# The first unit's loads and roots in whole pieces, the last store on GpSimd's queue, and a longer list of rank shifts

## The chip, the cores and the metric

The kernel runs on one core of a Trainium2 chip. TensorE (PE) multiplies matrices, VectorE (DVE) and ScalarE (ACT) work elementwise, GpSimd (POOL) and SyncE (SP) mostly issue DMAs; ACT can issue DMAs too. The metric is device time in microseconds; the kernel before took 703.22 us (median of 3 runs, 700.52 to 704.69).

## The reference, cut to what matters

Two blocks run one after the other. The first is a gated linear recurrence over 4 batches x 8 heads x 768 steps x 48 channels with a complex decay `a`, whose magnitude is limited first; the second is a dense block with a squared ReLU on the 3072 x 384 result.

```python
mag = np.sqrt(a_re * a_re + a_im * a_im)
scale = np.minimum(mag, 0.999) / (mag + 1e-06)
a_re_n, a_im_n = a_re * scale, a_im * scale
for t in range(S):                       # complex state S_re, S_im per head, 48 x 48
    new_re = ar * S_re - ai * S_im
    new_im = ar * S_im + ai * S_re
    S_re, S_im = new_re + k_t v_t^T, new_im
    y[:, :, t] = q_t @ S_re
x = y as (3072, 384)
out = max(x @ w_in, 0) ** 2 @ w_out      # w_in 384 x 2048, w_out 2048 x 384
```

## The kernel before, in words

The 3072 rows are cut into six units of 512 rows. A unit `n` has these stages. `load(n)` (line 880) brings `a`, `q`, `k` into the tiles `aq` and `v` into `v`; the eight heads lie in two halves `z` of four heads each. `chain(n)` (line 921) limits the magnitude of `a` (`roots`, `normalise`), multiplies the decays up over four neighbouring steps (`inner`, the DVE lines 1011 to 1019), scans them over the whole sequence by a turn on PE (`totals`), DVE products (`scan`) and a turn back (`back`, copied out by ACT at line 1246), and multiplies `q` and `k` by the result (`rest`, with `inverse`, `factors`, `twist`, `squares` and `apply`). `pairs(n)` (line 1356) turns the products on PE, forms scores (line 1419), masks them on DVE (line 1422) and mixes them into the columns `xT`. `dense(n, grp)` (line 1503) multiplies `xT` by `w1` (line 1511), squares the ReLU on ACT (lines 1542, 1543) and multiplies by `w2` (line 1557 in unit 0, line 1619 later, where sums of `w2` in the tile `T` save one product in eight).

The weights are first fetched whole and converted in pieces of 768 columns: an ACT pass (line 830, for the later pieces a second one at line 834) and two or three DVE passes (lines 836, 840, 843). Unit 0 shares DVE and ACT with this conversion. The fetches wait for a small copy (`gate`, line 908) that waits for unit 0's `a`.

No engine's order is written by hand. `step(engine, duration, reads, writes, function, rank)` and `dma(...)` only list the steps; `Plan.order` (line 531) then walks through planned time and, on each engine, starts among the steps that are ready the one with the smallest rank, and among equals the one listed first. A rank is a pair such as `(CHAIN, n)`, made into a number by 100 times the first plus the second: pairs of unit n have about 100 + n, the chain 200 + n, dense and the fetches 300 + n. Where the planner sees PE without work it adds multiplications of the identity (line 735) to keep it busy. `plan.shift` (line 1759) adds numbers to single ranks: `single` by the step's number in the list, `groups` by the number of the group of steps with one engine, one source line and one rank. The instructions of an engine run in the order that comes out.

In unit 0, and for `z = 0` alone, `load` cuts the four heads into two halves `u` of two heads, so that `a_re` (on SP's queue) and `a_im` (on ACT's) come in two DMAs each, and `roots` (line 938) does its eight steps twice on 384 columns, once for each half. The loads of `q` and `k` of unit 0 are listed as reading `("a", 1)`.

The last rows of the output are stored in halves of 192 columns (`rows`, line 1566): three of the four on SP's queue, the very last one, `(i, half) == (1, 0)`, on ACT's.

Of the kernel before, what the change touches and what calls it, by code (L numbers as in the profile page):

```python
# [621 lines left out]
def fast_path(ctx, tc, q, k, v, a_re, a_im, moe_w_in, moe_w_out, out, flag):  # L622
# [7 lines left out]
    W = 4  # L630
# [117 lines left out]
    def ac(n):  # L748
        return n / 1200.0 + 0.18
# [120 lines left out]
    def parts(n):  # L870

        t, got = n * L, []
        while t < (n + 1) * L:
            b, s = divmod(t, S)
            m = min(S - s, (n + 1) * L - t)
            got.append(((t - n * L) // W, m // W, b, s))
            t += m
        return got

    def load(n):  # L880
        rank = (CHAIN, n)
        for half, name, pair in ((0, "a", (a_re, a_im)), (1, "qk", (q, k))):
            for z in range(2):
                t = aq[z][:, half * Z:(half + 1) * Z].rearrange(
                    "p (r h x) -> p r h x", r=2, h=HH)
                late = []
                if half and (n == 1 or n > 2):
                    late = [("xT", (n - 1) % 2, NM - 1)]
                if half and n == 0:
                    late = [("a", 1)]  # L890

                cut = 2 if n == 0 and half == 0 and z == 0 else 1
                for u in range(cut):
                    for j, ap in enumerate(pair):
                        for p0, m, b, s in parts(n):
                            hs = slice(u * HH // cut, (u + 1) * HH // cut)
                            src = ap[b, z * HH + hs.start:z * HH + hs.stop, s:s + m * W, :]
                            src = src.rearrange("h (p c) d -> p h (c d)", c=W)
                            queue = act if n == 0 and half == 0 and j else sp
                            dma(queue, late,  # L900
                                [(name, z)] + ([(name, z, "r", j, u)] if n == 0 else []),
                                lambda t=t, p0=p0, m=m, j=j, src=src, queue=queue, hs=hs:
                                queue.dma_start(out=t[p0:p0 + m, j, hs], in_=src),
                                rank, m * 3072 // cut, 4.0 if n else 3.0, group=n)
            if n == 0 and half == 0:
                for z in range(2):
                    step("POOL", 0.2, [("a", z)], [("gate",)],
                         lambda z=z: pool.tensor_copy(out=gate[:, z:z + 1],
                                                      in_=aq[z][:, Z - 1:Z]), rank)
        t = vv[vs(n)].rearrange("p (i h d) -> p i h d", i=W, h=H)  # L910
        for i in range(W):
            b, s = divmod(n * L + i * C, S)
            src = v[b, :, s:s + C, :].rearrange("h (t c) d -> c t h d", c=W)
            for c in range(W):
                vrank = (CHAIN, 1) if n == 1 else (DENSE, 6 + n)
                dma(pool, [("xT", (n - (vs(n) == vs(n - 1))) % 2, NM - 1)] if n else [("gate",)], [("v", vs(n))],
                    lambda i=i, c=c, src=src: pool.dma_start(  # L917
                        out=t[32 * c:32 * c + 32, i], in_=src[c]), vrank, 32 * 1536, 4.0,
                    group=n)

    def chain(n):
# [15 lines left out]

        def roots(z):
            f0, f1, m2, t = col[z]
            if n:  # L940
                check("ACT", ac(Z), [("a", z)], key(z, 0, 1), lambda: act.activation(
                    out=ff[z][:, 0:Z], in_=A[z], func=AF.Square,
                    accum_out=sums[:, n, z:z + 1]), first)
            cut = 2 if n == 0 and z == 0 else 1
            size = Y // cut
            for u in range(cut):
                def k(*js, u=u):
                    return key(z, *js) if n else [("f", z, j, u) for j in js]

                def part(x, u=u):  # L950
                    return x[:, ts(u, size)]
                if n == 0:

                    if z == 0:
                        step("ACT", ac(size), [("a", z, "r", 0, u)], k(0),
                             lambda u=u: act.activation(
                                 out=part(f0, u), in_=A[z][:, ts(u, size)], func=AF.Square), first)
                    for r in range(z == 0, 2):
                        def square(r=r, u=u):
                            x = A[z][:, r * Y + u * size:r * Y + (u + 1) * size]  # L960
                            dve.tensor_tensor(out=part(col[z][r], u), in0=x, in1=x, op=ALU.mult)
                        step("DVE", tt(size), [("a", z, "r", r, u)], k(r), square, first)
                step("DVE", tt(size), k(0, 1), k(2) + key(z, 2),
                     lambda u=u: dve.tensor_tensor(
                         out=part(m2, u), in0=part(f0, u), in1=part(f1, u), op=ALU.add), first)
                step("ACT", ac(size), k(2), k(0), lambda u=u: act.activation(
                    out=part(f0, u), in_=part(m2, u), func=AF.Ln), first)
                step("ACT", ac(size), k(0), k(1), lambda u=u: act.activation(
                    out=part(f1, u), in_=part(f0, u), func=AF.Exp, scale=-0.5), first)
                step("ACT", ac(size), k(1), k(3), lambda u=u: act.activation(  # L970
                    out=part(t, u), in_=part(f1, u), func=AF.Square), first)
                step("DVE", tt(size), k(2, 3), k(3), lambda u=u: dve.scalar_tensor_tensor(
                    out=part(t, u), in0=part(m2, u), scalar=-0.5, in1=part(t, u),
                    op0=ALU.mult, op1=ALU.mult), first)
                step("DVE", tt(size), k(1, 3), k(3) + key(z, 3),
                     lambda u=u: dve.scalar_tensor_tensor(
                         out=part(t, u), in0=part(t, u), scalar=1.5, in1=part(f1, u),
                         op0=ALU.add, op1=ALU.mult), first)

        def normalise(z):  # L980
            f0, f1, f2, t = col[z]
# [584 lines left out]
    def rows(n, grp, i, o, half=None):  # L1566
# [2 lines left out]
        final = n == NU - 1 and grp == 1  # L1569
        if final and half is None:  # L1570
            return
        queue = (act if (i, half) == (1, 0) else sp) if final else pool
        if final:
            sl = ts(half, DH)
            dma(queue, [("ot", o, half)], [], lambda: queue.dma_start(
# [179 lines left out]
    for i in range(2 * NPIECE):  # L1755
# [1 line left out]
    verdict()  # L1757

    plan.shift(
        groups={77: 100.01, 80: 2.93, 100: -0.9, 159: -2.64, 161: 0.18, 232: 0.28, 234: 103.28,  # L1760
            258: 1.25, 297: 0.64, 352: 0.34, 354: 0.6, 372: 0.17, 394: -2.31},
        single={368: 0.46, 613: -197.29, 866: 8.98, 921: 0.46, 1273: -97.94, 1425: -0.29,
            1687: -97.83, 1759: 1.33, 1763: 98.01})
    with tc.manual_schedule():
        bad = plan.emit(flag[0:1, 0:1])
    return bad
# [53 lines left out]
```

## Time and profile before

| what | value |
|---|---|
| median of 3 runs | 703.22 us (700.52, 703.22, 704.69) |
| the profiled execution's own time | 704.69 us |
| its span in the profile | 702.97 us; 1.72 us lie around it |
| PE busy | 686.7 us (98%), of which 62.5 us identity (line 735) |
| DVE / ACT / POOL busy | 572.7 / 350.4 / 174.7 us |
| granted PE clock | 1.00 in nearly all 20 us windows, 0.83 from 80 to 100 us |

All times are microseconds from the span's start. A line of a group names line of the kernel, engine, operation, output<-input tiles, number of columns and count. The chain of waits goes back from the last instruction, at each step to what released it. In a table by windows the columns are the stretch, its length, the busy time of PE, PE's weight loads (PEld), DVE, ACT and POOL with the instructions in parentheses, the granted PE clock, the DMA engines' busy share, and GB/s.

### The profile page before, as it was taken

How to read it: one execution, taken by the hardware profiler on the slowest of the kernel's cores; microseconds unless marked ns; L12 is line 12 of the kernel's file. 1: busy time of each engine (PE TensorE's matmuls, PEld its weight loads, DVE VectorE, ACT ScalarE, POOL GpSimd, SP SyncE). 2: the span in 40 equal slices, each digit the busy share in tenths (PEclk: the TensorE clock that was granted, in tenths of full speed). 3: DMA queues.
4: the chain of work that ended last, by engine and by line, in shares of the span. 5: the costliest groups of instructions: out<-in, count | busy, mean ns of one | idle time of the engine just before them, and what ended most of it. 6: DMA issues, size and time to landing. Idle time of an engine off the chain costs nothing.

```text
span 703.0 us, 12562 instructions
## 1 busy us (share of the span) xinstructions
PE 686.7 (98%) x4572; PEld 623.3 (89%) x4572; DVE 572.7 (81%) x1177; ACT 350.4 (50%) x582; POOL 174.7 (25%) x334
## 2 busy tenths in 40 slices
PE   9998999999999999999999999999999999999996
PEld 9998888667778999998998898999989989989995
DVE  6989989999889689997898598998689998337721
ACT  7575379955575534376424557333657242132230
POOL 6502543052300003205044050033230033032100
PEclk9999989999999999999999999999999999999998
DMA  9740459130530004735037570037550035288600
GB/s 283 216 176 19 116 133 310 56 68 23 158 114 23 1 19 122 190 91 145 6 97 194 124 154 12 1 95 184 136 150 1 24 90 139 59 289 279 202 7 22
DMA packets 56679, 79.58 MB, mean 113 GB/s; under 512 B 11008, under 2 KB 38784, under 8 KB 56608
## 3 DMA queue, kind: packets, MB, share of 16 engines
q0 software_dynamic: 15232, 40.72, 19.2%
q1 hardware_dynamic: 37088, 32.89, 18.2%
q10 hardware_dynamic: 4288, 5.08, 2.7%
q8 instruction: 38, 0.62, 0.4%
q14 instruction: 33, 0.27, 0.1%
HBM read 48.76 MB, written 4.72 MB: 76 GB/s over the span
## 4 chain that ended last, share of the span: by engine, by line
PE 67%; DVE 20%; ACT 3%; issue 3%; DMA 3%; POOL 2%; SPq 1%; DVEq 0%; ACTq 0%; POOLq 0%
PE d L1511 26%; PE d L1619 22%; PE sc L1419 5%; PE tr L1447 3%; PE yp L1471 3%; PE d L1557 2%; DVE f L1299 2%; DVE f L1285 2%; PE yp L1475 2%; DVE f L1011 2%; PE tr L1511 2%; POOL T L917 1%; PE sc L1511 1%; DVE aq L1289 1%; DVE w L840 1%
## 5 line engine op out<-in xcount | busy, mean ns | idle before, releaser
L1511 PE MATMUL d<-xT,w 128*128 128x256 f32 x1056 | 235.5, 380 | 0.7 <-DVE ot L1643 0.7
L1511 PEld LDWEIGHTS d<-xT,w 128*128 128x128 f32 x1056 | 198.8, 190 | 28.7 <-DVE ot L1643 1.5
L1619 PE MATMUL d<-w,g 128*128 128x192 f32 x768 | 132.8, 327 | 0.0
L1619 PEld LDWEIGHTS d<-w,g 128*128 128x128 f32 x768 | 124.9, 190 | 1.6 <-issue 0.9
L1542 ACT ACTIVATE g<-d 128x512 f32<-128x512 f32 x88 | 52.3, 594 | 127.9 <-PE d L1511 94.3
L1340 POOL DMA_DIRECT2D KC<-f x160 | 78.5, 498 | 110.9 <-issue 47.4
L1580 POOL DMA_DIRECT2D out_dram<-ot x22 | 12.6, 572 | 241.8 <-DVE ot L1643 146.4
L1619 PE MATMUL d<-T,g 128*128 128x192 f32 x384 | 66.5, 327 | 0.3 <-DVE g L1634 0.3
L735 PE MATMUL d<-ident 128*128 128x128 f32 x530 | 62.5, 282 | 1.5 <-POOL ident masks.py:199 1.5
L1619 PEld LDWEIGHTS d<-T,g 128*128 128x128 f32 x384 | 62.8, 190 | 0.8 <-DVE g L1634 0.6
L735 PEld LDWEIGHTS d<-ident 128*128 128x128 f32 x530 | 61.9, 198 | 1.5 <-POOL ident masks.py:199 1.5
L917 POOL DMA_DIRECT2D v<-in_v_dram x80 | 46.4, 587 | 65.5 <-PE yp L1471 30.5
L1543 ACT ACTIVATE g<-g 128x512 f32<-128x512 f32 x96 | 60.6, 631 | 3.1
L1634 DVE TENSOR_TENSOR g<-g 128x512 f32<-128x512 f32 x64 | 43.0, 683 | 22.2 <-ACT g L1543 15.7
L1419 PE MATMUL sc<-QT 96*128 96x128 f32 x368 | 48.0, 285 | 0.8 <-ACT QT L1405 0.8
L1481 ACT COPY yt<-yp 112x512 f32<-112x512 f32 x24 | 26.2, 1091 | 44.5 <-PE yp L1475 44.5
L1419 PEld LDWEIGHTS sc<-QT 96*128 96x128 f32 x368 | 45.0, 198 | 2.7 <-issue 1.3
L1285 DVE TENSOR_TENSOR f<-aq,xn 128x384 f32<-128x384 f32 (+1 forms) x64 | 45.1, 748 | 2.3 <-ACT xn L1246 2.3
L1299 DVE TENSOR_TENSOR f<-aq 128x384 f32<-128x384 f32 (+1 forms) x64 | 45.0, 751 | 0.6
L1557 PE MATMUL d<-w,g 128*128 128x384 f32 x128 | 44.2, 488 | 0.2 <-DVE w L843 0.2
L1422 DVE TENSOR_TENSOR A<-sc,mask 128x512 f32<-128x512 f32 x45 | 29.9, 681 | 14.6 <-PE sc L1419 14.6
L1011 DVE TENSOR_TENSOR f<-aq 128x384 f32<-128x384 f32 x72 | 36.8, 552 | 0.8
(195 smaller groups left out, 989.5 us busy)
## 6 DMA issues: line engine op xcount, KB each, us to landing
QT<-aq SPq DMA_DIRECT2D x128, 64.0 KB, 2.2
f<-in_moe_w_in_dram POOLq DMA_DIRECT2D x8, 768.0 KB, 7.2
f<-in_moe_w_out_dram POOLq DMA_DIRECT2D x8, 768.0 KB, 6.3
KC<-f POOLq DMA_DIRECT2D x104, 48.0 KB, 2.4
out_dram<-ot POOLq DMA_DIRECT2D x22, 192.0 KB, 2.3
QT<-aq ACTq DMA_DIRECT2D x64, 64.0 KB, 2.4
v<-in_v_dram POOLq DMA_DIRECT2D x80, 48.0 KB, 3.3
xT<-yt SPq DMA_DIRECT2D x36, 96.0 KB, 2.5
```

The source lines that it names most:

```text
L735: plan = Plan(lambda b: pe.matmul(bank[b][:, 0:C], lhsT=ident, rhs=ident, start=True, stop=True), ["d2", "d1", "d0"], lambda ap: tc.nc.val ...
L917: lambda i=i, c=c, src=src: pool.dma_start(out=t[32 * c:32 * c + 32, i], in_=src[c]), vrank, 32 * 1536, 4.0,
L1011: dve.tensor_tensor(out=f, in0=a[:, :, :, c - 1], in1=a[:, j, :, c].unsqueeze(1).to_broadcast([C, 2, HH, D]), op=ALU.mult)
L1285: lambda j=j, r=r: dve.tensor_tensor(out=f4[:, j, r], in0=a[:, r], in1=over(j), op=ALU.mult), late[z])
L1299: lambda j=j, r=r, o=o: dve.tensor_tensor(out=o[:, :, :, r * D:(r + 1) * D], in0=qk[:, j], in1=a[:, r], op=ALU.mult), late[z])
L1340: lambda i=i, c=c, queue=queue: queue.dma_start(out=kc[32 * c:32 * c + 32, i], in_=nat[32 * i:32 * i + 32, c]),
L1419: pe.matmul(sa[:, j], lhsT=T[:, j, 1, h], rhs=T[:, j, 0, h], start=True, stop=True)
L1511: pe.matmul(ps, lhsT=w1[:, f // FP, m, ts(f % FP, C)], rhs=xT[:, n % 2, m, ts(grp, G)], start=(m == 0), stop=(m == NM - 1))
L1542: act.activation(out=o, in_=ps, func=AF.Relu)
L1543: act.activation(out=o, in_=o, func=AF.Square)
L1557: pe.matmul(ps, lhsT=gt[:, f % 2, ts(i, C)], rhs=w2[:, f], start=(f == 0), stop=(f == NF - 1))
L1619: pe.matmul(bank[b][:, 0:DH], lhsT=g4[:, r, j], rhs=w(j), start=first and j == 0, stop=last and j == NT - 1)
```

## The change

It does four things.

1. `load`: unit 0's `a` for `z = 0` comes in one DMA for `a_re` and one for `a_im`, not two each; unit 0's `q` and `k` are no longer listed as reading `("a", 1)`; the planner's latency for these loads is 1.8 in place of 3.0.
2. `roots`: unit 0's `z = 0` is done in whole steps of 768 columns, like `z = 1`.
3. `rows`: the very last store is issued by POOL in place of ACT.
4. `plan.shift`: all 22 old entries stay, renumbered where ten steps fewer stand ahead of them, and 15 are added. By numbering the steps of the kernel before, the new ones touch: `groups` 51 (the two ACT copies of unit 0's `back`, rank 199.99 to 301.96), 183, 190, 192, 217 (unit 2: the first closing DVE step of `roots`, line 972; ACT's check at line 999, to the front; `joined` after line 1011, by +0.69; `twist`, line 1045, to the back), 396 and 411 (unit 5: `joined` and the first step of `inverse`, line 1033, to the front); `single` 48 (one DVE pass of the conversion, line 840), 244 (a turn of unit 0's second pair, line 1401), 425 and 481 (two PE steps of unit 0's dense, lines 1511 and 1557), 584 (a small DVE step of unit 1's `scan`), 731 (the DVE mask of unit 1's first pair, second head, line 1422, rank 101 to 204.3), 809 (the last of the sums of `w2`, rank 101.5 to 301.97), 2212 (an ACT check of unit 5, line 1258).

```diff
@@ load
-                if half and n == 0:
-                    late = [("a", 1)]
-
-                cut = 2 if n == 0 and half == 0 and z == 0 else 1
-                for u in range(cut):
-                    for j, ap in enumerate(pair):
-                        for p0, m, b, s in parts(n):
-                            hs = slice(u * HH // cut, (u + 1) * HH // cut)
-                            src = ap[b, z * HH + hs.start:z * HH + hs.stop, s:s + m * W, :]
-                            src = src.rearrange("h (p c) d -> p h (c d)", c=W)
-                            queue = act if n == 0 and half == 0 and j else sp
-                            dma(queue, late,
-                                [(name, z)] + ([(name, z, "r", j, u)] if n == 0 else []),
...
-                                rank, m * 3072 // cut, 4.0 if n else 3.0, group=n)
+                for j, ap in enumerate(pair):
+                    for p0, m, b, s in parts(n):
+                        src = ap[b, ts(z, HH), s:s + m * W, :].rearrange(
+                            "h (p c) d -> p h (c d)", c=W)
+                        queue = act if n == 0 and half == 0 and j else sp
+                        dma(queue, late, [(name, z)] + ([(name, z, "r", j)] if n == 0 else []),
+                            lambda t=t, p0=p0, m=m, j=j, src=src, queue=queue:
+                            queue.dma_start(out=t[p0:p0 + m, j], in_=src),
+                            rank, m * 3072, 4.0 if n else 1.8, group=n)
@@ roots
-            cut = 2 if n == 0 and z == 0 else 1
-            size = Y // cut
-            for u in range(cut):
...
-                step("DVE", tt(size), k(0, 1), k(2) + key(z, 2),
-                     lambda u=u: dve.tensor_tensor(
-                         out=part(m2, u), in0=part(f0, u), in1=part(f1, u), op=ALU.add), first)
...
+            step("DVE", tt(Y), key(z, 0, 1), key(z, 2), lambda: dve.tensor_tensor(
+                out=m2, in0=f0, in1=f1, op=ALU.add), first)
+            step("ACT", ac(Y), key(z, 2), key(z, 0), lambda: act.activation(
+                out=f0, in_=m2, func=AF.Ln), first)
+            step("ACT", ac(Y), key(z, 0), key(z, 1), lambda: act.activation(
+                out=f1, in_=f0, func=AF.Exp, scale=-0.5), first)
+            step("ACT", ac(Y), key(z, 1), key(z, 3), lambda: act.activation(
+                out=t, in_=f1, func=AF.Square), first)
+            step("DVE", tt(Y), key(z, 2, 3), key(z, 3), lambda: dve.scalar_tensor_tensor(
+                out=t, in0=m2, scalar=-0.5, in1=t, op0=ALU.mult, op1=ALU.mult), first)
+            step("DVE", tt(Y), key(z, 1, 3), key(z, 3), lambda: dve.scalar_tensor_tensor(
+                out=t, in0=t, scalar=1.5, in1=f1, op0=ALU.add, op1=ALU.mult), first)
@@ rows
-        queue = (act if (i, half) == (1, 0) else sp) if final else pool
+        queue = (pool if (i, half) == (1, 0) else sp) if final else pool
@@ shift
-        groups={77: 100.01, 80: 2.93, 100: -0.9, 159: -2.64, 161: 0.18, 232: 0.28, 234: 103.28,
-            258: 1.25, 297: 0.64, 352: 0.34, 354: 0.6, 372: 0.17, 394: -2.31},
-        single={368: 0.46, 613: -197.29, 866: 8.98, 921: 0.46, 1273: -97.94, 1425: -0.29,
-            1687: -97.83, 1759: 1.33, 1763: 98.01})
+        groups={51: 101.97, 77: 100.01, 80: 2.93, 100: -0.9, 159: -2.64, 161: 0.18, 183: 98.76,
+            190: -200.92, 192: 0.69, 217: 103.2, 232: 0.28, 234: 103.28, 258: 1.25, 297: 0.64,
+            352: 0.34, 354: 0.6, 372: 0.17, 394: -2.31, 396: -101.12, 411: -201.73},
+        single={48: 0.43, 244: 2.93, 358: 0.46, 425: 4.98, 481: -297.85, 584: 0.23, 603: -197.29,
+            731: 103.3, 809: 200.47, 856: 8.98, 911: 0.46, 1263: -97.94, 1415: -0.29,
+            1677: -97.83, 1749: 1.33, 1753: 98.01, 2212: -0.63})
```

## The prediction

> **What bounds the kernel now.** I read the page's summary first, then the chain of waits from the start, then busy time by windows, then PE's, DVE's and the stores' timelines.
>
> ```profile
> PE 686.7 (98%) x4572; PEld 623.3 (89%) x4572; DVE 572.7 (81%) x1177; ACT 350.4 (50%) x582; POOL 174.7 (25%) x334
> ```
>
> PE is busy 98% of the span, but 62.5 us of that is the identity, and in PE's timeline the last identity runs at 98 us. So there are two regimes: a start in which PE waits for the first unit, and a PE stream behind it. The chain of waits through the start:
>
> ```profile
> 0.81 0.45 SPq L903
> 1.31 3.98 DMA aq<-in_a_re_dram
> 5.32 0.52 ACT f L956
> 5.84 0.42 ACT f L966
> 6.28 0.53 ACT f L968
> 6.84 0.53 ACT f L970
> ...
> 9.95 0.57 DVE f L976
> 10.54 0.84 ACT f L982
> 11.38 0.74 ACT f L989
> 12.15 0.85 ACT f L991
> 13.02 0.97 DVE f L993
> 14.07 1.77 DVE aq L996
> ```
>
> The reader is to see that the chain begins with the load of `a` and passes through the steps that are cut in two. After 13 us it stays on DVE almost without a break. The windows say the same (third busy column is DVE):
>
> ```profile
> 16.00:37.00 21.00, 21.00 (x190) 21.00 (x189) 20.20 (x38) 12.01 (x21) 10.80 (x18) 1.00 0.75 230
> 37.00:41.00 4.00, 4.00 (x38) 4.00 (x37) 2.14 (x6) 2.13 (x9) 0.00 (x0) 1.00 1.03 363
> 41.00:70.00 29.00, 27.03 (x238) 26.22 (x236) 27.41 (x81) 20.09 (x29) 4.11 (x9) 1.00 0.14 48
> ...
> 120.00:140.00 20.00, 19.80 (x74) 13.62 (x73) 19.62 (x38) 19.66 (x25) 0.71 (x1) 1.00 0.31 110
> ```
>
> Dense work on PE begins at 99.67 and waits once more for a converted weight:
>
> ```profile
> 99.67 2.86 PE L1511 MATMUL d<-xT,w 128*128 128x256 f32 x12
> 102.36 2.04 PE L1511 MATMUL sc<-xT,w 128*128 128x256 f32 x8
> 105.73 1.13 PE L1511 MATMUL tr<-xT,w 128*128 128x256 f32 x4 [1.32 <-DVE w L843]
> ```
>
> From 105.73 on, the gaps between multiplications in the trace sum to only 2.9 us (the longest 0.54). So what delays the start of the dense work delays the end; what only reorders DVE and ACT later costs or gains little unless PE runs dry.
>
> The Trainium skill, "Trainium Kernel Development and Optimization", in its Best Practices, tells the reader to judge PE by weight-load busy time and not by matmul busy time. By that rule the window from 120 to 140 has 6.4 us free (PEld 13.62 of 20), and a late start could be caught up there: the sum below would then be near 0.5 us. The rows decide otherwise. In the chain of waits 24 matmuls of 256 columns take 5.18 us (216 ns each) and 8 of 384 columns 2.58 us (322 ns). The window's 36 and 38 of these make 7.8 + 12.2 = 20.0 us: wide matmuls with no room between them.
>
> **The change part by part.** The sum is made against the profiled execution (704.69 us, span 702.97), which is 1.47 us above the median.
>
> Loads in whole. In the DMA records the two halves of `a_re` land at 3.97 and 5.29, those of `a_im` at 4.34 and 5.51. The whole arrays are the same bytes, first in the same two queues, so I put them at 5.3 and 5.5; a bound below is 5.0 (two issues of 0.46 us fewer). `z = 1` stays at 8.46 and 9.42: the load of `q` stands in SP's queue behind it now too, and issues about 0.5 us earlier. Unit 0's other `q` and `k` loads, issued at 3.99 and 5.31 after a completion, come earlier; nothing on the chain waits for them before 35 us, so nothing is counted.
>
> Roots in whole. A step of 768 columns takes 0.96 us on DVE and 0.84 on ACT (the rows of `z = 1`); one of 384 takes 0.56 and 0.52. After `a_im` at 5.5: square 0.96, add 0.96, three ACT steps 2.5, each with about 0.1 between: 10.2. Between them DVE waits for `z = 1` to land and does its two squares, to 10.4. Two closing steps of 0.96: 12.35. Then ACT's lines 982, 989, 991 (2.5) and line 993 at 14.95, against 13.02. If the planner puts `z = 1`'s own ACT steps first, line 993 comes at 16.6 instead, but DVE then does in the gap the two closing steps of `z = 1` that stood at 20.92 and 21.90: 16.6 + 0.96 - 13.98 - 1.92 = 1.66. So the chain behind is 1.65 to 1.93 us later. The 0.64 us of DVE time that four pairs of short steps cost more than whole ones is saved where DVE waits anyway. Nothing else is ready for DVE there: the first ACT conversion ends at 18.1. I take +1.65. Ends: 0 (a wait further on covers it: 37 to 41 has 1.9 us without DVE work, but that is the round trip over PE and ACT, which moves along) and +1.93.
>
> `back` of unit 0 (two copies of 0.48 us at 53.62 and 54.28) now has a rank behind the conversions. A pair of ACT conversions ready then (lines 830 and 834, 0.91 + 1.94 = 2.85 us, which ran at 56.91) goes first; behind the copies wait ACT's square (line 1109) and DVE's line 1285. DVE has converted pieces waiting and does one (0.55 + 0.96 + 0.96 = 2.5 us). So the chain of unit 0 is up to 2.85 us later and the conversions as much earlier. At 99.67 dense would start up to 1.65 + 2.5 later, at 103.8, but then without its waits: the 24 matmuls up to 106.9 need 5.2 us, so today's start is worth 101.7. The step adds between 0 and 0.5 (103.8 - 101.7 = 2.1, less 1.65): +0.4.
>
> The other ranks. Steps that stood alone among the ready ones do not move: lines 972 and 1045 of unit 2, unit 1's scan step. `joined` of unit 2 lets one 0.96 us step go ahead, the last sum of `w2` goes behind the normalising of unit 2, ACT's check (0.83 + 0.19 us) goes in front; unit 5's `inverse` goes ahead of a normalising step. Unit 5's `joined` and its check keep their neighbours. Each moves DVE or ACT by 1 us under a full PE stream: 0, and if that cover is gone 1 us each, four of them, at the most the PE gaps of 2.9 us in a gain. The two PE steps of unit 0's dense change places with other matmuls of the same stream: 0, and uncovered at the most the 0.6 us that an ACT pass behind one of them takes. The mask of unit 1's first pair goes behind the rest of `apply`; its mixing waits, PE has dense work of unit 0 (20 us of line 1557 between 167 and 213), so 0; its price uncovered is a rival below. The turn of unit 0's second pair and one pass of the conversion: 0, ends -0.5 and +1.
>
> The last store. The add ends at 696.35; ACT's issue takes 0.38 us and its landing 4.0:
>
> ```profile
> L1575 ACTq DMA_DIRECT2D out_dram<-ot x1: 378/378/378, 696.4 to 696.4; - x1
> ...
> L1580 POOL DMA_DIRECT2D out_dram<-ot x22: 539/568/687, 154.4 to 657.4; - x22
> ...
> DMA to landing us min/median/max: 2.1/2.3/6.6
> ```
>
> In the packet records most of it has landed at 698.0, one engine's part only at 700.37, behind instruction fetches of 8 and 16 KB; SP's closing waits then take 1.75 us, to 702.14, where POOL answers. POOL's issue is 0.57, so 0.19 later, and its landing by its own rows (192 KB) 2.1 to 2.3: up to 1.7 earlier. But POOL must now branch over the fallback path and drain behind this store. It did that early, from 673.18: 2.98 us to the next instruction, 0.43 of waits, 0.52 and a drain of 1.37, 5.3 in all. From 696.96 that ends at 702.3, against 702.14. So +0.2; ends -0.3 (a shorter drain) and +2.6 (a landing of 6.6).
>
> The Trainium skill, "DMA: Bandwidth & Descriptors", Issuing engine by pattern, gives a simple store to SP and calls the hardware path generally faster, with a first byte after 0.6 us against 1 on GpSimd's. By it the store would cost 0.4 us. No run here shows these two stores side by side yet.
>
> Sum: 1.65 + 0.4 + 0 + 0.2 = 2.25 us, 706.9 for the profiled execution, 705.5 from the median.
>
> **The rivals.** (a) The start is hidden: the conversions, not unit 0's chain, end last at 105.73, so a later `xT` costs nothing. For it speaks the wait of 1.32 us on line 843 there, against it that DVE does those conversions itself, behind the same late chain. Time: 703.2 + 0.2 + 0.3 = 703.7. (b) Slower: PE runs dry before 100 us and its clock falls. It is 0.83 from 80 to 100, worth 0.17 x 20 = 3.4 us, behind gaps of 3.5 us between 64 and 86. If unit 0's pairs come 4 us later and the planner's filling does not fit, such a stretch is paid once more: 705.5 + 3.4 = 708.9. It decides from some 3 us of further gaps; the mask of unit 1 waiting behind 5 us of `apply`, with PE's dense work used up, would cost as much. (c) Faster: the new orders close PE gaps. At the most 2.9 us behind 105 and 2 of the slow clock: 705.5 - 4.9 = 700.6. Against it: each gap has another releaser.
>
> **How the numbers follow.** A measurement of this kernel tells about 0.5%, 3.5 us, from no change: 699.7 to 706.7. Forecast 0.46 (own range 703.7 to 707.3), (a) 0.15, (b) 0.28, (c) 0.11. Slower: a fifth of the forecast's and five sixths of (b)'s: 0.09 + 0.23 = 0.32. Faster: half of (c): 0.06. Same 0.62. The range leaves out about a tenth on each side: 701.5 (inside (c)) to 709.5 (above (b)'s middle).
>
> **What would show it.** Line 993 of the first half at 14.9 to 16.6; dense starting at 103 to 104 with no wait on line 843; PE gaps behind it near 3 us; from the last add to the end 6.6 to 6.9 us. A clock under 0.83 before 100 us, or gaps over 5 us behind it, would say (b). The prediction is wrong if the planner's order in the first 100 us differs by more than these steps.

## The result and the profile after

The changed kernel takes 705.67 us (median of 20 runs, 702.98 to 707.63), the kernel before 703.35 in 20 runs beside them: ratio 1.0034, 95% interval 1.0023 to 1.0045. That is within 0.5%, and next to the 705.5 us forecast. But the forecast put 2.05 us of its sum into the start of the kernel and 0.2 into the store, and the runs below show it nearly the other way round.

The profiled execution takes 706.46 us with a span of 704.65, 1.68 longer than the span before. From `roots` on, a line of the changed kernel has a number 19 lower than in the kernel before, so line 993 is now 974, line 1511 is 1492, and the last store's line 1575 is 1556. The page's summary of the changed kernel:

```profile
PE 685.3 (97%) x4562; PEld 621.6 (88%) x4562; DVE 571.9 (81%) x1173; ACT 347.9 (49%) x578; POOL 176.3 (25%) x335
```

PE is 1.4 us less busy in a span 1.7 us longer. Its chain of waits through the start:

```profile
0.85 4.83 DMA aq<-in_a_im_dram
...
10.36 0.83 ACT junk L966 x2
11.19 0.74 ACT f L949
...
15.17 0.85 ACT f L972
16.05 0.97 DVE f L974
17.10 1.77 DVE aq L977
...
35.01 0.84 issue
35.86 0.36 DVE f L1020
```

The planner put the ACT steps of `z = 1` (lines 949 to 953, from 11.19) ahead of the first half's closing ones, so the first half's last step of `normalise` (line 974) begins at 16.05, 3.03 us later than before. Yet the scan behind it is earlier: its first step stood at 40.40 and stands at 37.26. The planner put conversions off: five DVE passes of them stood ahead of the scan before (lines 836 to 843), one stands there now. So the copy that the first turn on PE needs (`xn`) ends at 32.47 in place of 35.20, and the turn begins at 34.81 in place of 38.34. (Line 1020, formerly 1039, belongs to `inverse`; `twist`, line 1026, formerly 1045, begins at 36.24 in place of 35.74.) The windows of the changed kernel (the columns as in the prediction) show what that makes of the round trip:

```profile
16.00:37.00 21.00, 21.00 (x190) 21.00 (x190) 19.42 (x36) 14.28 (x29) 10.65 (x18) 1.00 0.75 226
37.00:41.00 4.00, 4.00 (x38) 4.00 (x37) 3.71 (x15) 3.94 (x9) 0.00 (x0) 1.00 1.04 377
41.00:70.00 29.00, 26.63 (x239) 25.97 (x239) 27.65 (x76) 16.53 (x22) 4.99 (x11) 1.00 0.16 54
...
120.00:140.00 20.00, 20.00 (x75) 13.80 (x75) 19.52 (x39) 19.17 (x23) 0.85 (x1) 1.00 0.27 95
```

Between 37 and 41 DVE worked 2.14 us before and works 3.71 now: the wait that stood there is gone. Dense work on PE, in PE's timeline of the changed kernel:

```profile
97.73 3.13 PE L1492 MATMUL d<-xT,w 128*128 128x256 f32 x12
100.70 1.12 PE L1492 MATMUL sc<-xT,w 128*128 128x256 f32 x4
103.99 2.40 PE L1492 MATMUL d<-xT,w 128*128 128x256 f32 x10 [2.17 <-issue]
106.56 1.13 PE L1492 MATMUL tr<-xT,w 128*128 128x256 f32 x4 [0.17 <-DVE w L843]
```

It begins 1.94 us earlier and then waits 2.34 us in place of 1.32. The second, short wait is for a converted weight. The first one has no releaser in the profile ("issue"). Two copies of unit 0's result into `xT` are issued shortly before:

```profile
100.24 1.17 SPq L1470 DMA_DIRECT2D xT<-yt  x2
```

The second of them, issued at 100.82, has landed at 103.90, and the weight load of the waiting multiplication starts at 103.96. In `e5_after_act` and `e11_after_fewer_id` (below) the same wait also ends 0.06 us behind the same landing (104.61 and 104.67; 101.23 and 101.29). So here PE waits for unit 0's own output and not for a conversion.

From 200 to 400 us PE's steps stand 0.2 to 0.35 us earlier than before; at 512 us two gaps put them 0.93 later, and they stay so. The rest of the 1.68 us is the end. First the last store's row among those that write the output, in the changed kernel:

```profile
L1556 POOL DMA_DIRECT2D out_dram<-ot x1: 565/565/565, 697.6 to 697.6; - x1
```

Then the rows of DMA issues in the last 10 us (count, KB, us from issue to landing), of the changed kernel and of the kernel before:

```profile
out_dram<-ot POOLq DMA_DIRECT2D x1, 96.0 KB, 4.0
```

```profile
out_dram<-ot ACTq DMA_DIRECT2D x1, 96.0 KB, 4.0
```

In both profiled executions the store lands 4.0 us after its issue. From the end of the last add to the end of the span it is 7.36 us now and was 6.61. In the changed kernel's instruction records POOL issues at 697.58. Its closing work beyond the branch begins with semaphore waits at 700.56, of which one goes on at 701.62, as the store lands; then come an instruction at 701.79 (0.54 us) and a drain of 1.45 us that ends at 703.81, behind SP's closing waits at 703.45. So POOL now ends last.

**A ledger for PE.** Since PE is nearly always busy, its end (here the start of its last multiplication) can be taken apart with three counts from each trace: the identity multiplications (0.112 us each from start to start), the gaps of over 0.1 us between multiplications behind 30 us, and what is left. The fifth column is the length of the stretches in which the records grant PE half its clock.

| kernel | PE's end | identities | gaps | half-clock stretch | rest |
|---|---|---|---|---|---|
| before | 695.64 | 530 = 59.4 | 7.73 | 6.83 | 628.5 |
| after | 696.57 | 520 = 58.2 | 10.06 | 6.83 | 628.3 |
| e1_start | 700.99 | 538 = 60.3 | 12.38 | 6.82 | 628.3 |
| e2_store | 696.44 | 530 = 59.4 | 8.85 | 3.41 | 628.2 |
| e3_ranks | 705.64 | 614 = 68.8 | 11.11 | 0 | 625.7 |
| e4_late_a | 696.32 | 530 = 59.4 | 9.73 | 3.41 | 627.2 |
| e5_after_act | 695.92 | 520 = 58.2 | 9.85 | 6.83 | 627.9 |
| e6_same_order | 696.92 | 530 = 59.4 | 8.70 | 6.83 | 628.8 |
| e7_no_unit5 | 694.37 | 520 = 58.2 | 9.64 | 0 | 626.5 |
| e8_store_sp | 694.52 | 530 = 59.4 | 7.21 | 6.83 | 627.9 |
| e9_fewer_id | 693.78 | 476 = 53.3 | 12.22 | 6.82 | 628.3 |
| e10_whole_fewer_id | 695.53 | 476 = 53.3 | 11.67 | 10.24 | 630.6 |
| e11_after_fewer_id | 693.58 | 484 = 54.2 | 13.10 | 0 | 626.3 |
| e12_order | 692.04 | 484 = 54.2 | 10.97 | 0 | 626.9 |

The rest is the same work: 627.9 to 628.8 with 6.8 us at half clock, 627.2 and 628.2 with 3.41, 625.7 to 626.9 with none. Of the 0.93 us that PE ends later after the change, the identities give -1.1, the gaps +2.3 and the rest -0.2.

One execution is not the kernel, though. `e2_store` and `e8_store_sp` have the PE order of the kernel before. In their profiles PE's steps are 0.7 and 0.5 us earlier than in its profile from 200 to 380 us, and behind 520 us 0.8 later and 1.1 earlier. A shift of under about 1 us between two profiles is therefore within what executions of one order differ by.

### The profile page after: what moved, and what is told of

The parts are those of the page before. It is cut to its first block, busy times and chain, and to the rows that moved or that the text cites. A ratio compares the mean times of both kernels' runs of the same rounds, so it can differ in the third digit from the quotient of the medians.

```text
span 704.6 us, 12517 instructions
## 1 busy us (share of the span) xinstructions
PE 685.3 (97%) x4562; PEld 621.6 (88%) x4562; DVE 571.9 (81%) x1173; ACT 347.9 (49%) x578; POOL 176.3 (25%) x335
## 4 chain that ended last, share of the span: by engine, by line
PE 67%; DVE 23%; issue 5%; DMA 2%; ACT 2%; SPq 1%; DVEq 0%; POOLq 0%; POOL 0%; ACTq 0%
PE d L1492 26%; PE d L1600 21%; PE sc L1400 5%; PE d L1538 3%; PE yp L1452 3%; PE tr L1428 3%; DVE f L1280 3%; DVE f L1266 3%; PE yp L1456 2%; PE tr L1492 2%; DVE aq L1270 1%; DMA aq<-in_a_im_dram 1%; PE sc L1492 1%; DVE f L992 1%; DVE aq L977 1%
## 5 line engine op out<-in xcount | busy, mean ns | idle before, releaser
L735 PE MATMUL d<-ident 128*128 128x128 f32 x520 | 60.5, 279 | 1.5 <-POOL ident masks.py:199 1.5
L735 PEld LDWEIGHTS d<-ident 128*128 128x128 f32 x520 | 59.9, 196 | 1.5 <-POOL ident masks.py:199 1.5
```

The costliest lines, as they stand in the source:

```text
L735: plan = Plan(lambda b: pe.matmul(bank[b][:, 0:C], lhsT=ident, rhs=ident, start=True, stop=True), ["d2", "d1", "d0"], lambda ap: tc.nc.val ...
```

## The experiments

Each ratio, with its 95% interval, is to runs of the kernel before on the same chip. It need not be the quotient of the two medians: for `e5_after_act` these are 703.41 and 703.37, with a ratio of 1.0009. Shown times in the traces are of one profiled execution each. All twelve kernels do the whole computation; the identity multiplications that four of them leave out write a bank that nothing reads.

**The start alone** (`e1_start`): parts 1 and 2 of the change, with the old list of ranks renumbered and the store on ACT.

```diff
-                cut = 2 if n == 0 and half == 0 and z == 0 else 1
-                for u in range(cut):
-                    for j, ap in enumerate(pair):
...
+                for j, ap in enumerate(pair):
...
-            cut = 2 if n == 0 and z == 0 else 1
-            size = Y // cut
...
+            step("DVE", tt(Y), key(z, 0, 1), key(z, 2), lambda: dve.tensor_tensor(
+                out=m2, in0=f0, in1=f1, op=ALU.add), first)
...
```

> The kernel before with the whole-piece loads and roots alone (old ranks, store on ScalarE's queue). Theory A, the one of the prediction: the load and roots steps make the start 1.65 to 1.9 us later and the end as much, ratio about 1.0024. Theory B, from the profile of after, where the dense work of units 1 to 3 stands no later than before: the planner puts other work into the hole, so the start costs under 0.5 us, ratio 0.999 to 1.0007.

Measured: 708.41 us, ratio 1.0074 (1.0053 to 1.0096), far over both. The ledger names gaps, 4.65 us more than before, one of 2.49 us at 79.4 and one of 1.37 at 127.3. So the order that the planner makes of the shorter list with the old ranks leaves PE waiting more.

**The store alone** (`e2_store`):

```diff
-        queue = (act if (i, half) == (1, 0) else sp) if final else pool
+        queue = (pool if (i, half) == (1, 0) else sp) if final else pool
```

> The kernel before with the last store on GpSimd's queue alone. Theory A: +0.2 us. Theory B, from the profile of after: the issue starts 0.3 us after the add and not 0.04, takes 0.57 and not 0.38, and GpSimd's closing drain ends 0.4 us behind SyncE's closing waits: from the end of the last add to the end of the span 7.3 us and not 6.6, so +0.5 to +0.8 us, ratio 1.0007 to 1.0011. If GpSimd's landing were what a 2.3 us row says, the end would come 1 us earlier, ratio 0.9985.

Measured: 705.72 us, ratio 1.0027 (1.0015 to 1.0039), 1.9 us. From the last add to the end it is 7.13 us. The store lands after 3.2 us, at 700.7, before POOL is past its branch at 701.0; POOL's drain ends at 703.45, 6.0 us behind the issue. The forecast of +0.2 falls.

**The ranks alone** (`e3_ranks`): the kernel before with its pieces cut, its store on ACT, and the 15 new ranks (renumbered).

```diff
-            258: 1.25, 297: 0.64, 352: 0.34, 354: 0.6, 372: 0.17, 394: -2.31},
...
+        groups={51: 101.97, 77: 100.01, 80: 2.93, 100: -0.9, 159: -2.64, 161: 0.18, 183: 98.76,
+            190: -200.92, 192: 0.69, 217: 103.2, 232: 0.28, 234: 103.28, 258: 1.25, 297: 0.64,
+            352: 0.34, 354: 0.6, 372: 0.17, 394: -2.31, 396: -101.12, 411: -201.73},
+        single={50: 0.43, 254: 2.93, 368: 0.46, 435: 4.98, 491: -297.85, 594: 0.23, 613: -197.29,
+            741: 103.3, 819: 200.47, 866: 8.98, 921: 0.46, 1273: -97.94, 1425: -0.29,
+            1687: -97.83, 1759: 1.33, 1763: 98.01, 2222: -0.63})
```

> The kernel before with the 15 new ranks alone (cut loads and roots, store on ScalarE's queue). Theory A: +0.4 us from the copies of unit 0's turn back, the others nothing, ratio 1.0005. Theory B: unit 5's ranks open a gap of 0.7 us in front of TensorE at 512 us and cost 0.8 us in the end, and the mask of unit 1 another 0.3 or so, ratio 1.0012 to 1.002. A gain of more than 0.5 us would say that the ranks speed up the start.

Measured: 712.72 us, ratio 1.013 (1.0108 to 1.0153): 9 us, not small. The ledger gives identities +9.4, gaps +3.4, rest -2.8. The groups of identity multiplications, of this kernel and of the kernel before (count, busy us, mean ns):

```profile
L735 PE MATMUL d<-ident 128*128 128x128 f32 x614 | 72.7, 281 | 1.5 <-POOL ident masks.py:199 1.5
```

```profile
L735 PE MATMUL d<-ident 128*128 128x128 f32 x530 | 62.5, 282 | 1.5 <-POOL ident masks.py:199 1.5
```

With the new ranks on the old steps the planner sees PE idle more often and fills that with 84 more multiplications, which PE then really does. So whole pieces alone cost 5 us, ranks alone 9, and both together 0.6 (`e5_after_act` below): their prices do not add, and a sum over the parts of a planner's input has no meaning here.

**A later `a`** (`e4_late_a`): two loads of 384 KB more on SP's and ACT's queues, ahead of unit 0's `a`, into a part of `xT` that is overwritten later; the order is untouched.

```diff
+    for pad_q, pad_src, pad_c in ((sp, q, 0), (act, k, 1)):
+        pad_q.dma_start(
+            out=xT[:, 0].rearrange("p m t -> p (m t)")[:, pad_c * 768:(pad_c + 1) * 768].rearrange(
+                "p (h x) -> p h x", h=HH),
+            in_=pad_src[0, 0:HH, 0:L, :].rearrange("h (p c) d -> p h (c d)", c=W))
```

> The kernel before with two more loads of 384 KB in front of a, one on each of the two queues (they fill a tile that is written again later; the order of all other work is unchanged). a lands about 2.5 us later (first half at 6.5, not 4.0). Theory A, that a late start passes to the end because VectorE has no hole to fill with the order as it stands: dense work starts 2.5 us later and the time is 2.5 us longer, ratio 1.0035. Rival, that the start is hidden behind the conversions, which a late chain does not hold up: under 0.5 us, ratio under 1.0007.

Measured: 705.49 us, ratio 1.0026 (1.0011 to 1.0041), 1.8 us. The step that is line 993 before begins at 15.89, 2.87 later, the first conversion behind the wait (line 840 before) at 40.39 in place of 39.39, and unit 0's turns at 64 us are 1.0 later. So 1.9 us of a delay at the start is lost on the way to 40 us, and what exceeds it passes. The time lies between the two expectations, and its interval (0.8 to 2.9 us) holds this 1.0 us.

**The whole change with the store back on ACT** (`e5_after_act`):

```diff
-        queue = (pool if (i, half) == (1, 0) else sp) if final else pool
+        queue = (act if (i, half) == (1, 0) else sp) if final else pool
```

> The changed kernel with the last store back on ScalarE's queue (whole pieces and new ranks stay). Theory A, the terms of the prediction: the store is worth 0.2 us, so this stays 2.1 us above before, ratio 1.003. Theory C, from the store alone (+1.9 us): the store is most of the change, and whole pieces with their new ranks cost only about 0.4 us, ratio 0.9995 to 1.0015; from the end of the last add to the end of the span some 5 to 6.5 us, not 7.1 to 7.4.

Measured: 703.41 us, ratio 1.0009 (0.9995 to 1.0022). Without the store the best estimate of the change is +0.6 us, and its interval holds 1. The last store's issue row in its last 10 us:

```profile
out_dram<-ot ACTq DMA_DIRECT2D x1, 96.0 KB, 2.1
```

It lands in 2.1 us, and from the last add to the end it is 5.17. The same stretch in all kernels whose last store is on ACT: 4.81, 5.10, 5.17, 5.26, 5.27, 5.54, 5.63, 5.74, 5.75, 5.91, and 6.61 in the profiled execution of the kernel before, which is the longest of eleven. On POOL it is 7.36 and 7.13. Median against the mean of these two: 5.54 to 7.25, 1.7 us.

**The whole pieces in the old order** (`e6_same_order`): the planner still plans the half pieces, but the second half's step does the whole piece and the first half's does nothing, so every other instruction keeps its place.

```diff
-                    out=part(f0, u), in_=part(m2, u), func=AF.Ln), first)
+                    out=part(f0, u), in_=part(m2, u), func=AF.Ln) if u == cut - 1 else None, first)
```

> The kernel before with the cut loads and roots merged to whole ones and every other instruction in its old place on its engine (so no new order comes with it). Theory A: line 993 of the first half starts at 14.9 to 15.1 instead of 13.02, VectorE's chain behind it is 1.65 to 1.9 us later, and dense work and the end with it: ratio 1.0024. Rival: the delay is taken up by waits further on, under 0.7 us, ratio under 1.001.

Measured: 704.46 us, ratio 1.0009 (0.9993 to 1.0024). Line 993 begins at 14.72, 1.70 later (the prediction had 14.95). DVE's timeline of the kernel before around the wait, and then of this kernel:

```profile
36.62 0.95 DVE L1033 SCALAR_TENSOR_TENSOR f<-f 128x768 f32<-128x768 f32 x1
39.39 0.95 DVE L840 SCALAR_TENSOR_TENSOR w<-w,w 128x768 uint32<-128x768 uint32 x1 [1.82 <-issue]
```

```profile
38.32 0.95 DVE L1035 SCALAR_TENSOR_TENSOR f<-f 128x768 f32<-128x768 f32 x1
39.63 0.95 DVE L840 SCALAR_TENSOR_TENSOR w<-w,w 128x768 uint32<-128x768 uint32 x1 [0.37 <-issue]
```

DVE reaches the wait 1.70 us later and leaves it 0.24 later: the wait has taken up 1.46. What holds it? PE's timeline of the kernel before and of this kernel, the first turn of unit 0 being line 1065 (1067 here):

```profile
34.32 4.18 PE L735 MATMUL d<-ident 128*128 128x128 f32 x36
38.34 0.82 PE L1065 MATMUL tr<-perm,xn 128*128 128x128 f32 x6
```

```profile
34.23 4.52 PE L735 MATMUL d<-ident 128*128 128x128 f32 x39
38.59 0.82 PE L1067 MATMUL tr<-perm,xn 128*128 128x128 f32 x6
```

The turn's input is ACT's copy `xn`, in ACT's timeline before and here:

```profile
34.69 0.51 ACT L1026 COPY xn<-aq 128x384 f32<-128x384 f32 x1 [5.32 <-DVE aq L1019]
```

```profile
36.39 0.51 ACT L1028 COPY xn<-aq 128x384 f32<-128x384 f32 x1 [5.31 <-DVE aq L1021]
```

It ends at 35.20 before and at 36.90 here. In both, the turn begins only when PE has worked off a run of identity multiplications that stands ahead of it in PE's fixed order. Dense work starts 0.58 us later than before, PE's steps are 0.88 later from 157 to 400 us, and PE ends 1.28 later. The interval of the time alone does not rule out the 1.65 us of the forecast; the trace does, with 0.24 left at this wait and 0.58 at the start of dense work.

**The unit 5 ranks taken back** (`e7_no_unit5`): as `e5_after_act`, without three of the new entries.

```diff
-            352: 0.34, 354: 0.6, 372: 0.17, 394: -2.31, 396: -101.12, 411: -201.73},
+            352: 0.34, 354: 0.6, 372: 0.17, 394: -2.31},
-            1677: -97.83, 1749: 1.33, 1753: 98.01, 2212: -0.63})
+            1677: -97.83, 1749: 1.33, 1753: 98.01})
```

> The changed kernel with the store on ScalarE's queue and without the three ranks of unit 5 (two groups and one check). If the gap of 0.7 us in front of TensorE at 512 us comes from them, it closes, and the matmuls behind 520 us stand 0.7 us earlier than with these ranks, ratio 0.001 below that of the changed kernel with the store on ScalarE's queue. If the gap comes from elsewhere it stays, and the ratio is the same.

Measured: 703.0 us, ratio 1.0007 (0.999 to 1.0024), not to be told from `e5_after_act`. The gap at 512 us (0.70 in the changed kernel, 0.38 there) is 0.11 here, but PE's lead over `e5_after_act` is the same in front of it and behind it (1.57 and 1.55 us). A gap of this size is under what these runs can tell.

**All last stores on SP** (`e8_store_sp`):

```diff
-        queue = (act if (i, half) == (1, 0) else sp) if final else pool
+        queue = sp if final else pool
```

> The kernel before with all four last stores on SyncE's queue. SyncE's rows land its stores of 96 KB in 1.6 us, but SyncE then has its branch (2.6 us) still in front of its closing waits: from the last add to the end 6 to 6.5 us. Against before, whose profiled run had 6.6 and whose order has shown 4.8 to 5.9 in other runs: 0 to +1.2 us, ratio 1.000 to 1.0017. If the landing is what counts and not the branch, it would be faster by 1 us, ratio 0.9985.

Measured: 705.72 us, ratio 1.0027 (1.0014 to 1.0039), as much as on POOL. The store lands in 2.2 us, but from the last add to the end it is 7.01: SP's closing work runs from its branch at 695.66, behind the issue, to 701.42. In `e5_after_act` it begins at 695.35, 1.3 us ahead of the end of the last add, and ends at 700.97. So the price is not how fast the store lands: here and in `e2_store` it has landed while the issuing engine is still at its branch. SP and POOL have 5.6 to 6.2 us of closing work of their own (branch, waits, drain), which starts only when they have issued, and when one of them issues the last store it ends last. With the store on ACT, POOL has done its own by 679 us in the kernel before, and SP begins its own before the last add has ended.

**The identity run shortened, pieces cut** (`e9_fewer_id`) **and whole** (`e10_whole_fewer_id`). The planner put 154 identity steps ahead of unit 0's first turn; 27 are left out. (Each turned out to be two multiplications in the trace: 530 became 476, so 6.0 us went and not the 3.0 meant.)

```diff
             many, b = self.fill.get(n, (0, None))
+            many -= 27 if n == 120 else 0
```

> The kernel before, with 27 of the 154 identity multiplications left out that stand in PE's order ahead of unit 0's first turn (line 1065); all else in its old place. Theory Q (what DVE waited for from 37.57 to 39.39 is PE's queue: the turn's input is ready at 35.2, but the turn stands behind a run of identity multiplications of 0.11 us each and begins at 38.34): the turn begins at 35.3 to 35.5, DVE's line 840 at 37.6 in place of 39.39, the scan's first step at 38.6 in place of 40.40, and dense work starts 1 to 1.8 us earlier than 99.67, unless conversions end last; time ratio 0.9975 to 0.999. Rival R (the wait is for a fetch that lands at 37.6 to 38.2, or is the round trip itself): line 840 within 0.3 us of 39.39, ratio 0.9995 to 1.0005.

> The kernel before with the four heads' pieces merged to whole ones and every other step in its old place (as in the run of whole pieces), and 27 of the 154 identity multiplications ahead of unit 0's first turn left out. Theory Q: the later roots now come through: the turn begins at 37.0 to 37.2 (its input is ready at 36.9), DVE's line 840 at 39.3, which is 1.7 later than in the run with the cut pieces and 27 fewer; dense work starts 1.3 to 1.7 us later than there; ratio to before 0.9995 to 1.0015, and 0.0015 to 0.0025 above that run. Rival R: line 840 at 39.4 to 39.7, and 0.0009 or less above that run.

Measured: cut pieces 702.24 us, ratio 0.9986 (0.997 to 1.0002); whole pieces 705.27 us, ratio 1.0016 (0.9996 to 1.0036). PE's timeline with cut pieces, then with whole ones:

```profile
32.00 0.27 PE L1066 MATMUL tr<-perm,xn 128*128 128x128 f32 x1
35.39 0.77 PE L1066 MATMUL tr<-perm,xn 128*128 128x128 f32 x5 [3.12 <-ACT xn L1027]
```

```profile
32.45 0.27 PE L1068 MATMUL tr<-perm,xn 128*128 128x128 f32 x1
37.39 1.32 PE L1068 MATMUL tr<-perm,xn 128*128 128x128 f32 x5 [4.67 <-ACT xn L1029]
```

Now PE waits for `xn`, as the prediction had believed that it did before. DVE's timeline, cut pieces and then whole ones:

```profile
36.75 0.95 DVE L1034 SCALAR_TENSOR_TENSOR f<-f 128x768 f32<-128x768 f32 x1
37.63 0.95 DVE L841 SCALAR_TENSOR_TENSOR w<-w,w 128x768 uint32<-128x768 uint32 x1
```

```profile
38.75 0.95 DVE L1036 SCALAR_TENSOR_TENSOR f<-f 128x768 f32<-128x768 f32 x1
39.63 0.95 DVE L841 SCALAR_TENSOR_TENSOR w<-w,w 128x768 uint32<-128x768 uint32 x1
```

The wait is gone in both, the conversion comes at 37.63 as theory Q had it, and the whole pieces are 2.00 us later, 0.30 more than the 1.70 of `e6_same_order`, where line 993 came 0.42 earlier; all of it is still there at 61 us. With the cover the whole pieces cost a ratio of 0.0009, without it 0.0030 (1.0016 over 0.9986). The intervals of the two runs overlap, so that it is the traces and not the times that show the delay passing. Nor is all of the 0.0030 the chain: in the profile of the whole pieces two half-clock stretches of together 10.24 us stand against 6.82.

**The same cut in the changed kernel** (`e11_after_fewer_id`): `e5_after_act` with 18 of the 142 identity steps ahead of its turn left out (36 multiplications, 4.0 us).

```diff
             many, b = self.fill.get(n, (0, None))
+            many -= 18 if n == 110 else 0
```

> The changed kernel with the last store on ACT and 18 of the 142 identity multiplications ahead of unit 0's first turn left out. Theory Q: its turn (line 1046) begins at 33.1 to 33.3 in place of 35.13, DVE's third step of line 1020 at 34.8 in place of 36.18, so the chain of unit 0 is 1.4 us earlier; ratio to before 0.998 to 1.0, 0.001 to 0.002 below the run with the store alone put back (1.0009). Rival (a) of the prediction, conversions end last before dense: the chain is 1.4 us earlier, but the wait for a converted weight at the start of dense grows by as much; ratio 1.0005 to 1.0013.

Measured: 702.71 us, ratio 0.9988 (0.9975 to 1.0). The third step of line 1020 (in `inverse`) begins at 34.86 in place of 36.18, and unit 0's chain is 1.35 us earlier than in `e5_after_act` up to 72 us. Behind that, PE's lead over `e5_after_act` of 3.4 us holds the absence of a half-clock stretch too. It grows to 4.03 and falls to 2.33 at 512 us. Rival (a) is not seen: at the start of dense work PE waits 1.65 us for the last copy into `xT` (2.09 in `e5_after_act`) and 0.20 for a converted weight in both.

**Two DVE steps put later** (`e12_order`): as `e11_after_fewer_id`, with the add that waits for unit 5's `a` (step 2125) put behind the DVE step that makes PE's next input (line 1616 there, step 1674), and line 978 (step 2135) behind the one after that. The rest keeps its order.

```diff
         order = self.order()
+        after, late, found = {2125: 1674, 2135: 1676}, [], []
+        for n in order:
+            hold = n in after or any(d in late for d in self.steps[n][2])
+            (late if hold else found).append(n)
...
+        order = found
```

> The run with the changed order, the store on ACT and 18 identity multiplications fewer, with two DVE steps of unit 5 put behind products of unit 4: the add of line 948 behind the next line 1616, line 978 behind the one after. There PE was 4.03 us ahead of the run without that cut at 478 us and only 2.33 at 514, with gaps of 0.61 and 0.70 us that end with DVE's line 1616, behind an add that waits for unit 5's a. Theory Q with this place as the next wait: both gaps go, PE keeps 3.4 to 3.8 of its lead, ratio to before 0.9965 to 0.998. Rival: unit 5's a lands too late for its chain anyway, the gaps come back later (unit 5's pairs, 578 to 610 us), ratio 0.9985 to 0.9995.

Measured: 701.19 us against 703.84 beside it, ratio 0.9965 (0.995 to 0.9981): faster than both kernels. PE's timeline around 510 us, of the changed kernel (in `e11_after_fewer_id` the two gaps are 0.61 and 0.70) and then of this one:

```profile
508.97 1.46 PE L1600 MATMUL d<-w,g 128*128 128x192 f32 x8
510.60 1.57 PE L1600 MATMUL d<-T,g 128*128 128x192 f32 x8 [0.16 <-DVE g L1615]
512.86 1.57 PE L1600 MATMUL d<-T,g 128*128 128x192 f32 x8 [0.70 <-DVE g L1615]
```

```profile
505.53 1.46 PE L1614 MATMUL d<-w,g 128*128 128x192 f32 x8
506.83 2.76 PE L1614 MATMUL d<-T,g 128*128 128x192 f32 x16
509.43 2.76 PE L1614 MATMUL d<-w,g 128*128 128x192 f32 x16
```

Both gaps are gone and do not come back later: PE's lead over `e5_after_act` is 3.9 us from 520 us to the end, 1.5 more than that of `e11_after_fewer_id`. The intervals of these two runs' ratios overlap; it is the trace that shows what this second edit adds. In the ledger the 3.9 us are -4.0 identities, +1.1 gaps and -1.0 rest.

## Why the prediction was right, and where only its number was

**The time** was right: 705.67 against 705.5, slower by less than 0.5%. That the number came out so well was luck: the start and the ranks were put at 2.05 us and measure 0.6, the store was put at 0.2 and measures 1.8, and the two errors cancel.

**Whole loads and roots, +1.65.** The delay itself was sized well: 1.70 at line 993 in the old order, and 16.05 in the changed kernel, the second of the two orders that the prediction gave. What failed is the sentence that the wait between 37 and 41 us "is the round trip over PE and ACT, which moves along". It did not: the turn stood behind identity multiplications with its input ready 3.1 us before, and PE's own queue, not the chain, set its time. `e6_same_order` shows the 1.46 us taken up there, `e4_late_a` shows the same for a later load, and the traces of `e9_fewer_id` and `e10_whole_fewer_id` show that the delay passes once the identities are out of the way. The prediction had that bound (0) and set it aside without looking at what PE did before the turn. In the changed kernel the planner put 142 identity steps there in place of 154 and moved conversions back, so the scan came 3.1 us earlier.

**`back` behind the conversions, +0.4.** The near effect came as written: the ACT pair goes first, the two copies (line 1227) come at 53.78, and DVE does a conversion in the gap. But they stood behind a scan that was 3 us earlier. Dense work began at 97.73, not at 103 to 104, and its waits grew in place of vanishing. Of the 2.05 us of these two terms PE's steps show nothing clear between 200 and 400 us: 0.2 to 0.35 earlier than before in the changed kernel, 0.25 to 0.4 later in `e5_after_act`.

**The other ranks, 0.** PE's steps lose some 1.2 us from 400 to 520 us (from 0.2 to 0.35 early to 0.93 late). The gap of 0.70 at 512 us is the largest piece; there two more DVE steps of unit 5's chain stand ahead of the products that PE waits for than before. But `e5_after_act` has the same order and loses nothing over the same stretch (0.39 later than before at 380 us, 0.28 behind 520), so this loss is the one execution's and not shown to be the ranks'. All that is not the store comes to 0.0009 (-0.0005 to 0.0022), 0.6 us, where 2.05 was forecast.

**The last store, +0.2.** Measured: 1.9 us alone, and 1.8 as the difference between the change with it and without it (1.0034 less 1.0009). The failing step is the base: the sum was made against one profiled execution. Its store landed after 4.0 us, behind instruction fetches, SP's closing waits went on only then (700.38), and its end was 6.61 us long, where ten other ends on ACT are 4.81 to 5.91. Against their median of 5.54 that is 1.1 of the 1.5 us missed. The row did say 4.0, against 2.1 to 2.3 for POOL's own stores, and that row alone should have been asked whether it was usual. The way in which POOL becomes last was right (branch, waits, drain), but took 6.2 us from the issue to the end of the drain (6.0 in `e2_store`), not 5.3.

**The two rules.** The Trainium skill, "Trainium Kernel Development and Optimization", Best Practices, judges the distance to PE's peak by the multiply work done and by weight-load busy time, not by matmul busy time. As the prediction applied it, a late start would be caught up from 120 us on. The traces answer that: in `e6_same_order` PE is 0.58 us late at the start of dense work and 0.88 late from 157 to 400 us, and in `e9_fewer_id` a lead of 3.31 us at 100 us is still 3.26 at 380, with weight loads at 13.6 to 13.8 us of 20 in the profiles of both kernels. Nothing was caught up. By the first-byte times of the Trainium skill's "DMA: Bandwidth & Descriptors", Specifications, the store was worth an estimated 0.4 us; measured it is 1.9. On SP, which the same page's Issuing engine by pattern gives for simple stores, it costs the same 1.9. The landing took 2.2 us there and did not decide.

**The rivals.** (a) was right that the start is hidden, and wrong about by what: identity multiplications. In the changed kernel conversions do not end last at the start of dense work either: PE waits there 2.17 us for unit 0's own `xT` and 0.17 for a conversion (1.65 and 0.20 with the identities cut). (b) did not come: the half-clock stretch is 6.83 us long in both profiles. (c) did not come: the gaps grew by 2.3 us.

**What stays open.** Of the 15 new ranks only the three of unit 5 were tried by themselves. Why some executions have a half-clock stretch and others none isn't settled, and so not how much of the gain of `e11_after_fewer_id` is its earlier chain. By the ledger against `e5_after_act` it is 0.8 us of identities less gaps and 1.6 of the rest.

## What to carry to other kernels

Before a delay is passed down a chain, look at what the engine that takes the next step does just before it: filler work in a fixed order holds a step as firmly as a missing input. It hides a delay up to the wait that it makes (here 1.5 of 1.70 us), and costs that wait where the input is early. A stretch at the end of a kernel that depends on a single landing is read from several executions or several like stores, not from one; and the last store belongs on an engine whose own closing work behind it does not end last (here ACT and not POOL or SP). A planner's filler and orders are part of the price: with ranks fitted to another list of steps, two changes that cost 5 and 9 us alone cost 0.6 together.

## What the runs showed of the hardware that was not expected

The records grant PE half its clock for stretches of 3.41 us or twice that, beginning between 36 and 102 us, in most profiled executions, and in four of the fourteen (`e3_ranks`, `e7_no_unit5`, `e11_after_fewer_id`, `e12_order`) not at all before the last microseconds. By the ledger's last column PE ends some 0.2 to 0.5 us later for each microsecond of it (rest 625.7 to 626.9 without, 627.2 and 628.2 with 3.41 us, 627.9 to 628.8 with 6.8, 630.6 with 10.24). The mean granted clock over a kernel's runs goes roughly with it, though it also counts half clock behind PE's last work: 0.998 for `e11_after_fewer_id` and `e12_order`, 0.994 for the changed kernel, 0.992 for `e10_whole_fewer_id`. In `e9_fewer_id` and `e10_whole_fewer_id` such a stretch begins at 36.5 and 37.4, within 1.1 us of the end of a PE gap of 3.12 or 4.67 us; in the profiles of the two kernels, no PE gap in the 10 us ahead of such a stretch is over 0.85 us.

The last store of 96 KB landed on ACT's queue in 2.1 to 2.3 us in nine of eleven profiles, in 3.6 in `e12_order` and in 4.0 in the kernel before. In these two, 135 of its 144 packets were done early, and the other nine were written only from 0.1 us behind the end of an instruction fetch of 16 KB (699.31 in the kernel before, 695.34 in `e12_order`).
